# The second MLP matrix converted later, with a two-step threshold, wider loads of the mixed rows and one more buffer in two rings

## The chip, the cores and the metric

One core of a Trainium2 chip runs one program, start to end. The metric is the device time of one execution in microseconds (us), the median over the runs shown. The engines are named as the profile names them: PE (TensorE, with PEld for its weight loads), DVE (VectorE), ACT (ScalarE), POOL (GpSimd) and SP (SyncE), whose queue issues nearly every DMA of this program.

## The reference

The input `x` has 8 sequences of 3136 positions and 256 channels. Two layers are computed in float32:

```python
X = np.fft.rfft(x, axis=1)
Yr = Xr @ w_r - Xi @ w_i + b_r;  Yi = Xr @ w_i + Xi @ w_r + b_i
Y* = sign(Y*) * max(|Y*| - 0.01, 0)            # soft threshold
y  = np.fft.irfft(Yr + 1j * Yi, n=3136, axis=1)

mixed = real(fft(fft(y, axis=1), axis=2));  u = y + mixed
un = (u - mean(u)) / sqrt(var(u) + 1e-6)
out = u + max(un @ w_ch1, 0) @ w_ch2           # 256 -> 1024 -> 256
```

The MLP matrices `w_ch1` and `w_ch2` reach the program as raw 8-byte words and are turned on the chip into pairs of float32 values, a high and a low part.

## The kernel before

**Work and stages.** All heavy products are matrix multiplies on PE. Float32 accuracy comes from splitting an operand into a high part (type fp32r) and a low part (the remainder) and adding three products, `mm3` (L154 to L157). Eight sequences `b` go through three stages. Stage 1 (`p1`, L371) does the first half of a Fourier transform over positions (49 x 64 positions) and stores it to DRAM (`ad`). Stage 2 works in four quarters `q` of 8 frequencies each: `p2_f2` (L438) finishes the transform and makes the tiles Xh, Xl (and sums Xsh, Xsl), `p2_w` (L510) multiplies by the complex weights, adds the bias and applies the soft threshold into `Y`, `p2_mix` (L553) does the transform over channels and stores `mq` to DRAM as `md`, `p2_yt` and `p2_g2` (L648, L686) begin the inverse transform and store `bev` to DRAM as `bd`. Stage 3 takes groups of 3 or 4 position tiles: `p3_norm` (L718) loads `bf` from `bd` and `mt` from `md`, ends the inverse transform in PSUM (`g_g`), adds `mt` into `ut` and computes mean and variance; `p3_tr` transposes `ut` into `uth`, `utl`; `p3_mlp1` and `p3_mlp2` are the MLP (`h`, then `o`), and the result leaves from `ut`.

**Order.** Each stage of each sequence is a Python generator that yields a due time in units of T; a heap calls the one that is due next, and a scheduler that simulates the engines then fixes the order of every engine's instructions. At run time each engine follows its own fixed order and waits for semaphores. Stage 1 of the first sequence fills the time 0 to 1 T, stage 2 of the first sequence begins at 1 T, that of the second at 1.77 T (START1), stage 3 of sequence 0 at about 2 T. From there on the stages of neighbouring sequences overlap.

**The conversion.** `weights()` (L845) has eight pieces: four of `w1` (due from 1.14 T, L127) and four of `w2` (due from 1.56 T, step 0.05 T, L128). A piece loads 512 KB of raw words (L858) and runs `split_double` (L170): one ACT instruction (L179), six on DVE (L180, L182, L184, L185, L188, L190), a copy on ACT (L194) and two subtractions or additions on POOL (L196, L197). Its scratch tiles use the rings `mt` and `ut`. The raw words of `w2` lie in the tiles Xh and Xl (one buffer each), which hold the spectra of even quarters at other times. Behind the four pieces of `w1`, `center()` (L262) takes the mean out of it.

**The threshold.** `p2_w` adds bias and the product `ks` to the product in PSUM with one DVE instruction that writes `y1` (L544), clips `y1` to [-0.01, 0.01] into `m` (L546, DVE), and subtracts (L547: on DVE for the first sequence and where `o` is 0, else on POOL). PSUM has 8 banks: 4 for the tag `g` (every product outside the MLP), 2 for `h`, 2 for `o`.

**Loads of the mixed rows.** `p3_norm` loads `mt` for each pair of tiles: per source one DMA for the rows in rising order (L750) and one for each tile of the falling rows (L752), into a ring of 2 buffers.

Of the kernel before, what the change touches and what calls it, by code (L numbers as in the profile page):

```python
# [133 lines left out]
def spectral_block(ctx: ExitStack, tc: tile.TileContext, x, w_ri, b_ri, w1, w2,  # L134
# [78 lines left out]
    def load_consts():  # L213
# [504 lines left out]
    def p3_norm(b):  # L718
# [7 lines left out]
        def load_bf(m, n):  # L726
# [5 lines left out]
            return bf  # L732
        nxt = None
        for gi, (g0, z) in enumerate(groups[b % 2]):
            t0, T3 = clock3(b, g0)
            for i, n in parts_of[z]:
# [10 lines left out]
                mt = sb.tile([128, 2, D], F32, tag="mt", bufs=2, name="mt")  # L747
                for r, (bb, n2) in enumerate(sources(m)):
                    mpn, mmn = (d[0:NH].rearrange("(a n2) d -> a n2 d", n2=N2) for d in m_dram[bb])
                    nc.sync.dma_start(out=mt[32 * r:32 * r + 32, :n], in_=mpn[:, n2:n2 + n, :])  # L750
                    for j in range(n):
                        nc.sync.dma_start(out=mt[64 + 32 * r:96 + 32 * r, j], in_=mmn[:, 48 - n2 - j, :])  # L752
                if b and gi == i == 0:
                    yield t0 + T3 * (NRM + TURN)
# [8 lines left out]
                va.tensor_add(ut[:, :n], g[:, :w].rearrange("p (n d) -> p n d", d=D), mt[:, :n])  # L763
# [163 lines left out]
```

## Time and profile before

| what | value |
|---|---|
| median of the runs shown | 1908.15 us (three runs: 1908.15, 7055.32, 1907.27) |
| the profiled execution's own time | 1905.15 us |
| its span, first to last instruction | 1903.4 us |
| PE busy | 1838.9 us (97%) |
| DVE, ACT, POOL busy | 1255.0, 847.7, 706.1 us (66%, 45%, 37%) |
| mean granted TensorE clock | 0.983 |

The page cuts the span into 40 slices of 47.6 us. In the first four, PE is busy 5, 7, 7 and 6 tenths and the granted clock stands at 7, 9, 9 and 6 tenths; from the fifth slice on both are 9 tenths or more. A line with "[3.22 <-POOL ...]" says how long the engine sat idle before that instruction and what ended the wait. Matmuls are pipelined, and their busy times overlap.

### The profile page before, as it was taken

What the parts mean: (1) busy time and instruction counts of PE and PEld (TensorE: products, weight loads), DVE (VectorE), ACT (ScalarE), POOL (GpSimd) and SP (SyncE); (2) the same over time, 40 slices, a digit from 0 to 9 for tenths busy, and PEclk for the clock granted to TensorE, in tenths of its full rate; (3) what the DMA queues carried; (4) which work ended last, traced back from release to release, by engine and by line L of the source; (5) the groups of instructions that cost most, each with busy time, mean ns of one, the idle gap of its engine ahead of it and who ended that gap; (6) DMA issues with size and microseconds to landing.
All of it is one profiled execution on the core that took longest, in us unless ns stands there. A gap on an engine that the chain in (4) does not pass through costs nothing.

```text
span 1903.4 us, 34682 instructions
## 1 busy us (share of the span) xinstructions
PE 1838.9 (97%) x12123; PEld 1690.0 (89%) x12123; DVE 1255.0 (66%) x2726; ACT 847.7 (45%) x1892; POOL 706.1 (37%) x1093
## 2 busy tenths in 40 slices
PE   5776999999999999999999999999999999999999
PEld 4665999999999999989999999998999999998998
DVE  2885877767666766767766766766766776665443
ACT  2554545444544444444444544444454443443322
POOL 0565544343434334344323544324443332323110
PEclk7996999999999999999999999999999999999999
DMA  7775643354433545245443543435434342224110
GB/s 205 213 207 164 162 136 116 103 162 135 124 115 109 151 120 149 83 121 145 121 143 94 160 134 107 127 92 158 140 99 114 100 116 83 73 77 117 58 38 26
DMA packets 163716, 233.03 MB, mean 122 GB/s; under 512 B 27662, under 2 KB 107606, under 8 KB 163542
## 3 DMA queue, kind: packets, MB, share of 16 engines
q1 hardware_dynamic: 163542, 230.82, 42.8%
q8 instruction: 96, 1.57, 0.3%
q14 instruction: 78, 0.64, 0.1%
HBM read 127.95 MB, written 102.76 MB: 121 GB/s over the span
## 4 chain that ended last, share of the span: by engine, by line
PE 84%; DMA 5%; DVE 5%; SPq 2%; ACT 1%; issue 1%; POOL 1%; DVEq 0%; ACTq 0%; POOLq 0%
PE o L156 9%; PE o L155 9%; PE h L155 9%; PE o L157 9%; PE h L157 9%; PE h L156 9%; PE g_f L478 5%; PE g_w L155 3%; PE g_w L157 3%; PE g_w L156 3%; PE g_g L155 2%; PE g_yt L673 2%; PE g_g L156 2%; PE g_g L157 2%; PE g_ut L797 2%; PE g_mix L604 1%
## 5 line engine op out<-in xcount | busy, mean ns | idle before, releaser
L819 DVE SCALAR_TENSOR_TENSOR hl<-h,hh 128x512 fp32r<-128x512 f32 (+1 forms) x416 | 273.1, 657 | 335.9 <-ACT hh L818 334.2
L818 ACT ACTIVATE hh<-h 128x512 fp32r<-128x512 f32 (+1 forms) x416 | 238.5, 573 | 465.0 <-PE h L157 430.3
L156 PE MATMUL o<-w2h,hl 128*128 128x256 f32 x1568 | 427.7, 283 | 4.7 <-DVE hl L819 4.4
L157 PE MATMUL o<-w2h,hh 128*128 128x256 f32 x1568 | 421.6, 279 | 0.0
L155 PE MATMUL o<-w2l,hh 128*128 128x256 f32 x1568 | 391.2, 284 | 0.6 <-ACT hh L818 0.6
L155 PE MATMUL h<-utl,w1h 128*128 128x512 f32 (+1 forms) x832 | 324.4, 390 | 0.0
L157 PE MATMUL h<-uth,w1h 128*128 128x512 f32 (+1 forms) x832 | 317.7, 382 | 0.0
L156 PE MATMUL h<-uth,w1l 128*128 128x512 f32 (+1 forms) x832 | 317.4, 381 | 0.0
L156 PEld LDWEIGHTS o<-w2h,hl 128*128 128x128 f32 x1568 | 295.4, 188 | 11.2 <-DVE hl L819 6.1
L157 PEld LDWEIGHTS o<-w2h,hh 128*128 128x128 f32 x1568 | 295.2, 188 | 3.6
L155 PEld LDWEIGHTS o<-w2l,hh 128*128 128x128 f32 x1568 | 282.6, 189 | 12.8 <-ACT hh L818 0.8
L152 POOL TENSOR_TENSOR bl<-bf,bh 128x512 fp32r<-128x512 f32 x104 | 129.1, 1241 | 289.9 <-ACT bh L757 286.4
L152 POOL TENSOR_TENSOR xl<-xf,xh 128x512 fp32r<-128x512 f32 (+1 forms) x75 | 99.7, 1329 | 210.5 <-ACT xh L405 198.2
L157 PEld LDWEIGHTS h<-uth,w1h 128*128 128x128 f32 x832 | 156.3, 188 | 23.9
L155 PEld LDWEIGHTS h<-utl,w1h 128*128 128x128 f32 x832 | 156.6, 188 | 14.2
L156 PEld LDWEIGHTS h<-uth,w1l 128*128 128x128 f32 x832 | 156.7, 188 | 14.0
L478 PEld LDWEIGHTS g_f<-tff,af 98*128 98x128 f32 x1024 | 144.5, 197 | 19.8 <-issue 11.9
L478 PE MATMUL g_f<-tff,af 98*128 98x100 f32 x1024 | 151.0, 276 | 9.7 <-DMA tff<-c_tf 9.3
L152 POOL TENSOR_TENSOR Xl<-xx,Xh 128x400 fp32r<-128x400 f32 (+1 forms) x96 | 101.9, 1063 | 92.0 <-ACT Xh L492 42.2
L152 POOL TENSOR_TENSOR Xsl<-xs,Xsh 128x200 fp32r<-128x200 f32 x120 | 76.1, 635 | 103.4 <-ACT Xsh L492 90.8
L763 DVE TENSOR_TENSOR ut<-g_g,mt 128x512 f32<-128x512 f32 x104 | 68.3, 657 | 69.1 <-PE g_g L157 40.9
L772 POOL TENSOR_SCALAR vv<-ag 128x2 f32<-128x2 f32 x104 | 27.2, 261 | 205.4 <-DVE ag L769 182.7
(162 smaller groups left out, 3788.2 us busy)
## 6 DMA issues: line engine op xcount, KB each, us to landing
bd<-bev SPq DMA_DIRECT2D x128, 196.0 KB
bf<-bd SPq DMA_DIRECT2D x184, 128.0 KB
out_dram<-ut SPq DMA_DIRECT2D x92, 256.0 KB
af<-ad SPq DMA_DIRECT2D x60, 392.0 KB
xf<-in_x SPq DMA_DIRECT2D x176, 128.0 KB
ad<-ev SPq DMA_DIRECT2D x176, 128.0 KB
md<-mq SPq DMA_DIRECT2D x112, 192.0 KB
mt<-md SPq DMA_DIRECT2D x416, 32.0 KB
```

The source lines that it names most:

```text
L152: gp.tensor_sub(out_, full, hi.bitcast(F32))
L155: te.matmul(o, lh, rl, start=start, stop=False)
L156: te.matmul(o, ll, rh, start=False, stop=False)
L157: return te.matmul(o, lh, rh, start=False, stop=stop)
L478: f2_mm[b, q, ui] = te.matmul(o, afs[s][:, ui * D + k * 128:ui * D + k * 128 + 128], tfs[s][:, ui].rearrange("p (c j) -> p c j", c=2), sta ...
L604: te.matmul(o, eh[:, e, ui], cs, start=e == 0, stop=False)
L673: te.transpose(gt[:100, (v * 2 + o) * 128:(v * 2 + o + 1) * 128], y[:, o, place].rearrange("p c j -> p (c j)"), ident)
L763: va.tensor_add(ut[:, :n], g[:, :w].rearrange("p (n d) -> p n d", d=D), mt[:, :n])
L772: gp.tensor_scalar(vv[:, :n], ag[:, :n, 1:2], 1.0, EPS, op0=ALU.mult, op1=ALU.add)
L797: te.transpose(gv[:, k, j * 128:(j + 1) * 128], ut[:, j, k * 128:(k + 1) * 128], ident)
L818: sc.activation(hh[:, :w], h[:, :w], AF.Relu)
L819: va.scalar_tensor_tensor(hl[:, :w], h[:, :w], 0.0, hh[:, :w].bitcast(F32), op0=ALU.max, op1=ALU.subtract)
```

## The change

- The soft threshold becomes two DVE instructions and one on ACT. L545 (numbers of the changed file) adds bias and `ks` and writes the sum back into the same PSUM tile; ACT makes r = max(sum - 0.01, 0) from PSUM (L549); DVE takes min(sum + 0.01, r) into `Y` (L550). POOL has no part in it any more. `y1` and `m` are gone.
- `mt` is loaded once for a group of up to 4 tiles (`load_mt`) into one buffer, a quarter of a group's time ahead of its use, and the falling rows of a group in one DMA with a negative step; the first group is loaded in two cuts.
- The ring `ut` has 7 buffers in place of 6, `bev` 3 in place of 2.
- The pieces of `w2` are due from 1.73 T in steps of 0.07 T. Their raw words lie in `uth` and `utl`, two buffers each, so that all four fit at a time; those tiles hold the spectra of quarters 1 and 3 of the first sequence before, and the transposed `ut` of stage 3 after. The scratch tile of a conversion is in the ring `hh`.

```diff
-W2_AT, W2_STEP = 1.56, 0.05
+W2_AT, W2_STEP = 1.73, 0.07
...
-    UTB = 6
+    UTB = 7
...
-        tf = tmp("mt", 2, F32)
+        tf = tmp("hh", 2, F32)
...
+    va.memset(lam_t, -LAM)
...
-                    y1 = sb.tile([128, 8, S], F32, tag="y1", bufs=2, name="y1")
-                    va.scalar_tensor_tensor(y1, gw, bias[:, c, o:o + 1], ks, op0=ALU.add, op1=ALU.add)
-                    m = sb.tile([128, 8, S], F32, tag="m", bufs=1, name="m")
-                    va.tensor_scalar(m, y1, -LAM, LAM, op0=ALU.max, op1=ALU.min)
-                    (va if b == 0 or o == 0 else gp).tensor_sub(y[:, o, :, c, :], y1, m)
+                    va.scalar_tensor_tensor(gw, gw, bias[:, c, o:o + 1], ks, op0=ALU.add, op1=ALU.add)
...
+                    r = sb.tile([128, 8, S], F32, tag="r", bufs=1, name="r")
+                    sc.activation(r, gw, AF.Relu, bias=lam_t)
+                    va.scalar_tensor_tensor(y[:, o, :, c, :], gw, LAM, r, op0=ALU.add, op1=ALU.min)
...
-                bev = sb.tile([98, 512], F32, tag="bev", bufs=2, name="bev")
+                bev = sb.tile([98, 512], F32, tag="bev", bufs=3, name="bev")
...
+        def load_mt(g0, z):
+            mt = sb.tile([128, 4, D], F32, tag="mt", bufs=1, name="mt")
+            cut = 2 if g0 == 0 else z - 1 if g0 + z == NM else z
+            for i, n in ((0, cut), (cut, z - cut))[:1 + (cut < z)]:
+                for r, (bb, n2) in enumerate(sources(g0 + i)):
+                    mpn, mmn = (d[0:NH].rearrange("(a n2) d -> a n2 d", n2=N2) for d in m_dram[bb])
+                    nc.sync.dma_start(out=mt[32 * r:32 * r + 32, i:i + n], in_=mpn[:, n2:n2 + n, :])
+                    nc.sync.dma_start(out=mt[64 + 32 * r:96 + 32 * r, i:i + n],
+                                      in_=mmn[:, 49 - n2 - n:49 - n2, :][:, ::-1])
+            return mt
...
+            if gi:
+                yield t0 + T3 * (NRM - 0.25)
+                mt = load_mt(g0, z)
...
-            tag, bufs = (("W2", "W3") if j < 4 else ("Xh", "Xl"))[j % 2], 1
+            tag, bufs = (("W2", "W3") if j < 4 else ("uth", "utl"))[j % 2], 1 + j // 4
...
-            if j + 1 < 4 or j >= 4 and j + 1 < 8:
+            if j + 1 < 4 or 4 < j < 7:
                 load(j + 1)
...
                 load(4)
+                load(5)
```

The scheduler moves many instructions. Three places matter here.

The DVE queue where the conversion of `w2` begins, in the kernel before; `cv_w_...` are its scratch tiles, `raw_w` its raw words, `y`, `m` and `Y` the threshold of quarter 3, and `mq` the channel mix of quarter 2:

```order
L271 TENSOR_TENSOR wc<-w1h,g_mean 128x512 x2
L184 TENSOR_SCALAR cv_w_ut<-raw_w_1169 128x512
L623 COPY mq<-mq 100x4x127
L544 SCALAR_TENSOR_TENSOR y_1210<-g_w,bias,ks 128x400
L180 TENSOR_SCALAR cv_w_mt<-cv_w_mt 128x512
L546 TENSOR_SCALAR m<-y_1210 128x400
L182 TENSOR_SCALAR cv_w_mt<-cv_w_mt 128x512
L409 COPY ev<-g_f_1241 128x512
L547 TENSOR_TENSOR Y<-y_1210,m 128x8x50
L185 TENSOR_TENSOR cv_w_ut<-cv_w_ut,cv_w_mt 128x512
```

And the same queue in the changed kernel, around the last threshold of quarter 3:

```order
L545 SCALAR_TENSOR_TENSOR g_w<-g_w,bias,ks 128x400
L550 SCALAR_TENSOR_TENSOR Y<-g_w,r 128x8x50
L617 TENSOR_TENSOR mq<-g_mix,mq 100x1
L620 TENSOR_TENSOR mq<-mq 100x4x64 x2
L585 SCALAR_TENSOR_TENSOR ef<-Y,mask 128x8x25 x2
L184 TENSOR_SCALAR cv_w_ut<-raw_w_1342 128x512
L180 TENSOR_SCALAR cv_w_hh<-cv_w_hh 128x512
L182 TENSOR_SCALAR cv_w_hh<-cv_w_hh 128x512
L185 TENSOR_TENSOR cv_w_ut<-cv_w_ut,cv_w_hh 128x512
L626 COPY mq<-mq 100x4x127
```

Before, all four pieces stand among the thresholds of quarter 3 and ahead of that quarter's `mq`; now no piece stands ahead of the last threshold, three stand ahead of quarter 3's `mq`, and the fourth behind it.

The SP queue where the raw words of `w2` are loaded, in the changed kernel; `af` is the input of the second sequence's stage 2, `bd` the store of the first sequence's inverse transform:

```order
L288 DMA xf<-in_x 64x512 x3
L460 DMA af<-ad_107 98x1024
L709 DMA bd_109<-bev 98x512
L288 DMA raw_w_1342<-in_w 128x2x512
L288 DMA raw_w_1344<-in_w 128x2x512
L288 DMA tif<-c_ti 100x392
L460 DMA af<-ad_107 98x1024
L709 DMA bd_109<-bev 98x512
L288 DMA raw_w_1521<-in_w 128x2x512
L288 DMA raw_w_1579<-in_w 128x2x512
```

The four loads stand close together, and the first can only issue once quarter 3's products have read `uth`; before, two stand behind quarter 2's products and the others each wait for a piece that is done.

The DVE queue at the first normalisation of stage 3, in the changed kernel; `ut` is the sum of the inverse transform and `mt`, `st` and `ag` its statistics, and `raw_w_1579` the fourth piece of `w2`:

```order
L545 SCALAR_TENSOR_TENSOR g_w<-g_w,bias,ks 128x400 x2
L550 SCALAR_TENSOR_TENSOR Y<-g_w,r 128x8x50
L776 TENSOR_TENSOR ut<-g_g_1662,mt 128x512
L776 TENSOR_TENSOR ut<-g_g_1690,mt 128x512
L184 TENSOR_SCALAR cv_w_ut<-raw_w_1579 128x512
L781 BN_STATS st<-ut 128x6
L550 SCALAR_TENSOR_TENSOR Y<-g_w,r 128x8x50
L781 BN_STATS st<-ut 128x6 x3
L185 TENSOR_TENSOR cv_w_ut<-cv_w_ut,cv_w_hh 128x512
```

Before, this stretch had the same work without any piece of the conversion in it.

## Rows read from the trace of the kernel before

**Rows 1.** Engines by stretch of the span: busy us (instructions), clock, DMA.
```profile
core 0: us, PE busy (x) PEld busy (x) DVE busy (x) ACT busy (x) POOL busy (x), PEclk, DMA share, GB/s
62.00:84.00 22.00, 17.17 (x95) 13.18 (x94) 22.00 (x41) 13.37 (x33) 13.77 (x15) 1.00 0.72 204
84.00:121.00 37.00, 35.04 (x197) 28.54 (x195) 27.01 (x57) 20.13 (x58) 21.04 (x25) 1.00 0.61 175
121.00:152.00 31.00, 19.56 (x90) 14.84 (x91) 30.66 (x49) 16.84 (x36) 20.21 (x13) 0.81 0.70 205
152.00:167.00 15.00, 11.40 (x59) 9.86 (x60) 7.96 (x16) 10.00 (x27) 10.02 (x9) 0.73 0.71 199
167.00:191.00 24.00, 16.32 (x56) 14.06 (x55) 9.99 (x24) 8.26 (x15) 10.77 (x20) 0.63 0.55 154
200.00:600.00 400.00, 400.00 (x2703) 371.50 (x2702) 284.26 (x621) 190.03 (x424) 163.45 (x247) 1.00 0.45 128
1100.00:1350.00 250.00, 249.00 (x1668) 229.81 (x1667) 172.54 (x373) 115.79 (x256) 100.40 (x147) 1.00 0.43 122
```

**Rows 2.** Waits of PE from 200 us on: us in total, times, longest.
```profile
PE o L156 <- DVE hl L819: 4.4, 4, 1.4
PE g_yt L673 <- DVE utl L149: 0.7, 1, 0.7
```

**Rows 3.** DVE groups in 50 to 134 us: busy us, mean ns of one, idle before.
```profile
L547 DVE TENSOR_TENSOR Y<-y,m 128x400 f32<-128x400 f32 x14 | 11.9, 853 | 0.2
L544 DVE SCALAR_TENSOR_TENSOR y<-g_w,bias,ks 128x400 f32<-128x400 f32 x13 | 8.2, 628 | 2.5 <-PE g_w L157 2.5
L546 DVE TENSOR_SCALAR m<-y 128x400 f32<-128x400 f32 x14 | 8.0, 573 | 0.2
```

**Rows 4.** DVE in order of time, 120 to 166 us: start, us.
```profile
120.78 0.43 DVE L184 TENSOR_SCALAR cv_w_ut<-raw_w 128x512 int32<-128x512 int32 x1 [3.50 <-DMA raw_w<-in_w]
...
122.33 0.36 DVE L546 TENSOR_SCALAR m<-y 128x400 f32<-128x400 f32 x1
...
127.82 1.43 DVE L546 TENSOR_SCALAR m<-y 128x400 f32<-128x400 f32 x1
...
165.47 1.21 DVE L623 COPY mq<-mq 100x508 f32<-100x508 f32 x1
```

**Rows 5.** POOL in order of time, at 127 us.
```profile
127.58 1.44 POOL L196 TENSOR_TENSOR cv_w_ut<-cv_w_ut,w2h 128x512 f32<-128x512 f32 x1
```

**Rows 6.** The conversion's tiles cv_w_ut, then cv_w_mt, in 121 to 152 us.
```profile
121.00:152.00 31.00, 12.47 (x16) 2.47 (x4) 10.10 (x7) 0.81 0.70 205
...
121.00:152.00 31.00, 8.17 (x12) 2.49 (x4) 0.81 0.70 205
```

**Rows 7.** Groups of the whole span by shape, on ACT and POOL.
```profile
L547 POOL TENSOR_TENSOR Y<-y,m 128x400 f32<-128x400 f32 x56 | 63.1, 1127 | 107.7 <-DVE m L546 105.7 <-DMA mt<-md 1.1
L535 ACT COPY ks<-g_w 128x400 f32<-128x400 f32 x64 | 31.5, 493 | 37.6 <-PE g_w L157 37.3
```

**Rows 8.** PE in order of time, 133 to 191 us.
```profile
133.16 0.34 PE L157 MATMUL g_w<-Xh,wdh 128*128 128x400 f32 x1
...
178.85 0.79 PE L155 MATMUL g_g<-bl,invh 128*128 128x512 f32 x1 [3.22 <-POOL Y L551]
...
185.15 1.11 PE L797 MATMUL g_ut<-ident,ut 128*128 128x128 f32 x4 [3.80 <-DVE ut L763]
...
191.03 0.39 PE L155 MATMUL h<-utl,w1h 128*128 128x512 f32 x1
```

**Rows 9.** SP's DMA issues in order of time, 114 to 175 us.
```profile
114.98 0.92 SPq L286 DMA_DIRECT2D raw_w<-in_w  x2
...
167.85 0.51 SPq L629 DMA_DIRECT2D md<-mq  x1
...
173.31 1.26 SPq L730 DMA_DIRECT2D bf<-bd  x2
```

**Rows 10.** DVE group of the sum from PSUM, in 600 to 1600 us.
```profile
L544 DVE SCALAR_TENSOR_TENSOR y<-g_w,bias,ks 128x400 f32<-128x400 f32 x69 | 43.3, 628 | 9.2 <-PE g_w L157 9.1
```

**Rows 11.** SP's waits over the span: us in total, times, longest.
```profile
SPq L750 <- DVE ut L763: 165.9, 53, 8.3
```

More of the change, by code (lines that the diff above doesn't have):

```diff
@@ L219, in load_consts @@
         behind("x", out=KF["wr"], in_=w_v[0])
-        wi = sb.tile([128, 2, D], F32, tag="mt", bufs=2, name="wi")
+        wi = sb.tile([128, 2, D], F32, tag="mt", bufs=1, name="wi")
         behind("x", out=wi, in_=w_v[1])
@@ L237, in load_consts @@
         sc.copy(cs[:, 0, 1, 0:1], t[:, 0, 128:129])
-        inv = sb.tile([128, 128], F32, tag="mt", bufs=2, name="inv_f")
+        inv = sb.tile([128, 128], F32, tag="mt", bufs=1, name="inv_f")
         nc.sync.dma_start(out=inv, in_=c_inv)
@@ L254, in spectral_block @@
         va.memset(t[:, :, 0:1], 0.0)
-    eps_t = cp.tile([128, 1], F32, name="eps_t")
+    two_t = cp.tile([128, 2], F32, name="two_t")
+    eps_t, lam_t = two_t[:, 0:1], two_t[:, 1:2]
     va.memset(eps_t, EPS)
+    va.memset(lam_t, -LAM)
     mlp_w = {}
@@ L542, in p2_w @@
                             done.add(("w", b))
-                    y1 = sb.tile([128, 8, S], F32, tag="y1", bufs=2, name="y1")
-                    va.scalar_tensor_tensor(y1, gw, bias[:, c, o:o + 1], ks, op0=ALU.add, op1=ALU.add)
-                    m = sb.tile([128, 8, S], F32, tag="m", bufs=1, name="m")
-                    va.tensor_scalar(m, y1, -LAM, LAM, op0=ALU.max, op1=ALU.min)
-                    (va if b == 0 or o == 0 else gp).tensor_sub(y[:, o, :, c, :], y1, m)
+                    va.scalar_tensor_tensor(gw, gw, bias[:, c, o:o + 1], ks, op0=ALU.add, op1=ALU.add)
+                    if b == q == o == c == 0:
+                        sb.tile([128, 32], F32, tag="gap", bufs=1, name="room")
+                    r = sb.tile([128, 8, S], F32, tag="r", bufs=1, name="r")
+                    sc.activation(r, gw, AF.Relu, bias=lam_t)
+                    va.scalar_tensor_tensor(y[:, o, :, c, :], gw, LAM, r, op0=ALU.add, op1=ALU.min)
             if q == 0:
@@ L746, in p3_norm @@
                 nxt = load_bf(*tiles[0]) if tiles else None
[L747 to L754, printed above, removed]
+                if gi == i == 0:
+                    mt = load_mt(g0, z)
+                    if b:
+                        yield t0 + T3 * (NRM + TURN)
                 bh = sb.tile([128, 512], F32R, tag="bh", bufs=2, name="bh")
@@ L762, in p3_norm @@
                 ut = sb.tile([128, 2, D], F32, tag="ut", bufs=UTB, name="ut")
[L763 removed]
+                va.tensor_add(ut[:, :n], g[:, :w].rearrange("p (n d) -> p n d", d=D), mt[:, i:i + n])
                 st = sb.tile([128, 2, 6], F32, tag="st", bufs=2, name="st")
```

## Prediction

> **What bounds the kernel now.** I read the engines by stretch first [rows 1]. From 200 to 600 us PE is busy 400.00 of 400, from 1100 to 1350 it is 249.00 of 250, both at the full clock of 2.4 GHz. The waits of PE from 200 us on [rows 2] are a handful; the largest sum is 4.4 us. So from about 191 us, where the first MLP product `h` runs [rows 8], to the end PE is the bound. The change adds no matrix product and takes none away, so those 1712 us can hardly become shorter. What can move is the start.
>
> There the same table shows DVE. In 62 to 84 us it is busy 22.00 of 22 while PE is busy 17.17. In 121 to 152 us it is busy 30.66 of 31 while PE has 19.56, at a clock of 0.81. From 152 to 191 us nobody is full: PE 11.40 of 15 and 16.32 of 24, clock 0.73 and 0.63. That is a chain of waits: quarter 3's last product at 133.16 us [rows 8], its `mq` copied at 165.47 us [rows 4], the `md` stores issued from 167.85 us and the second `bf` pair at 173.31 us [rows 9], PE's wait of 3.22 us for POOL at 178.85 us (the low part of `bf`; the row names the memset right behind it) and of 3.80 us for `ut` at 185.15 us [rows 8], and `h` at 191.03 us. PE's work of 121 to 191 us, each busy time multiplied by its clock, is 19.56 x 0.81 + 11.40 x 0.73 + 16.32 x 0.63 = 34.4 us at full clock. 70 - 34.4 = 35.6 us is all that can be had there, 4.8 us in 62 to 84 us, and 2.0 us in 84 to 121 us, where PE is busy 35.04 of 37.
>
> **The change part by part.** The sum is made against the profiled execution, 1905.15 us; the median of the runs stands 3.0 us above it, and I forecast the median.
>
> *Conversion of `w2`.* Its DVE work in 121 to 152 us is 12.47 + 8.17 = 20.64 us for four pieces [rows 6], 5.2 us a piece and two thirds of what DVE does there. In the new order no piece stands ahead of quarter 3's last threshold, three still stand ahead of quarter 3's `mq`, the fourth behind it. The three only change places with the thresholds; since DVE has no gap in the stretch, just the fourth leaves the path to `mq`: -5.2 us, with 0 as the other end (if PE, ACT or a transfer sets that end as soon as DVE gives way) and -12 us if the thresholds' earlier end also pulls forward what hangs on them.
>
> *The raw words.* Before, the first piece waits 3.50 us for them with DVE idle [rows 4], issued at 114.98 us and used at 120.78 us, 5.8 us later [rows 9, 4]. That idle time goes. Now their load issues behind quarter 3's last product. DVE has about 3.3 us of its own until it reaches the first piece (a sum, ACT's step, a minimum, two `mq` steps and two `ef`, by the durations below and some 0.75 us each for the pairs), so about 5.8 - 3.3 = 2.5 us of new idle time is late next. Behind that waiting instruction stand the copies that free the `g_mix` tiles, and PE's mix waits for them. Net -1.0 us; the ends are -3.5 (the loads land in time) and +2.5 us (the old wait was hidden).
>
> *The threshold.* Before: a sum of 628 ns, a clip of 573 and a subtraction of 853 [rows 3]. The last two come to 1.43 us. The new minimum reads one PSUM tile and one SBUF tile as the sum does, so I give it 0.63 us; it is not in this trace, and its bounds are the 628 ns of the sum and the 853 ns of the subtraction. ACT's step has the shape of the `ks` copy, 493 ns [rows 7]. In the new order sum and minimum often stand next to each other, so DVE idles up to 0.49 us in between. A product thus saves 1.43 - 0.63 = 0.80 us at best and 0.31 at worst; I take the middle, 0.55. Four products lie in 62 to 84 us and four in 121 to 152 us, where DVE is the bound: 8 x 0.55 = -4.4 us, ends -6.4 and 0 (the worst case with a minimum as long as the subtraction leaves 0.09 each).
>
> Why the old pair was long is seen in two rows: the same clip took 0.36 us at 122.33 us and 1.43 us at 127.82 us [rows 4], the latter while POOL ran a subtraction from 127.58 us for 1.44 us [rows 5]. The Trainium skill, SBUF — State Buffer, section "Who interferes with whom", says that a DVE instruction with two SBUF inputs, or in its two-port mode, can be blocked for the whole of a GpSimd instruction, and one with at most one SBUF input outside that mode is not. By that rule the minimum never stretches and its 0.63 us stands; were it to stretch as the subtraction did, the eight products would give back 8 x 0.22 = 1.8 us. The rows agree with the rule here. The skill's VectorE: DVE Perf Modes, section on the TRN2 errata, speaks against the gain: its cost of an instruction is 58 cycles from SBUF but 120 from PSUM, so without a GpSimd instruction beside them clip and subtraction are an estimated 0.27 + 0.48 us and the minimum 0.54, a gain of only 0.2 us, which ACT's step would eat; by it this term would be about 0.
>
> *A PSUM bank held longer.* It was free 0.63 us after the product; now after 0.63 + 0.49 + 0.63 = 1.75 us. In the first sequence, where PE has nothing but `g` tiles, some of the 16 products will stall PE: +1.5 us, ends 0 (no stall) and +6 (a third of 16 x 1.12).
>
> Later there is room. DVE runs 69 sums in 600 to 1600 us [rows 10], 16 to a sequence, so a sequence takes 232 us; it allocates about 125 `g` tiles (the loops of the three stages), one in 1.85 us, and with four banks one comes round after 7.4 us. 1.1 us more for 16 of 125 tiles should not be seen. There DVE saves little, POOL loses 63.1 us of subtractions [rows 7], ACT gains 112 x 0.49 = 55 us, and none of them is the bound. 0, ends -3 and +3 us.
>
> *The fourth piece in the first normalisation.* 5.2 us of DVE among the statistics of the first two tiles. DVE is busy 9.99 of 24 us there [rows 1], so most of it fits into waits: +1.0 us, ends 0 and +5.2.
>
> *Loads of `mt`, rings.* SP waits 165.9 us in total to reload `mt` [rows 11], off PE's path. Fewer DMAs and one more buffer for `ut` and `bev` shorten waits that other work covers; if that cover went, the 3.80 us before `ut` [rows 8] would show it. 0, ends -1 and +2.
>
> *The clock.* PE's instructions of 121 to 191 us lose 47.28 - 34.4 = 12.9 us to the lower clock, and the clock was lowest where PE waited most. Shorter waits should give back some: -1.5 us, ends 0 and -6.
>
> Sum: -5.2 - 1.0 - 4.4 + 1.5 + 0 + 1.0 + 0 - 1.5 = -9.6 us. 1905.15 - 9.6 = 1895.55, and with the 3.0 us to the median 1898.5 us.
>
> **The rivals.**
>
> *Nothing is gained.* The conversion stays ahead of quarter 3's `mq` with three of its four pieces, and between 152 and 191 us no engine is full, so transfers and SP's queue may set the end; the DMA engines are 0.71 busy at 152 to 167 us [rows 1], and the raw words of all four pieces now load behind 133 us. Against it speaks the DVE stretch without a gap. Price: the two DVE terms (9.6 us) go and the rest stays: 1908 us.
>
> *More is gained.* The thresholds of quarter 3 end without any conversion between them, and PE's transposes and the inverse transform follow at once, while DVE converts in what are now PE's stretches. From the last product to `mq` it took 165.47 - 133.16 = 32.3 us, some 10 us of it thresholds, pieces and stretched copies that would be gone. The -12 end of the first term with the -6 of the clock: -9.6 - 6.8 - 4.5 = -21 us, 1887 us.
>
> *Slower: the raw words come too late.* One mechanism at one place: SP issues in order and stops at the first raw load until quarter 3's last product; behind it stand the input of the second sequence's stage 2 and the stores of the inverse transform, and on DVE everything behind the first piece. For it speaks the position of the loads; against it that loads stood in SP's queue before as well. If the raw words cost their 5.8 us in full, the fourth piece its 5.2 us, the banks 1.5 us, and only the threshold's 4.4 us are gained, that is +8.1 us: 1916 us. It decides from a DVE wait above 5 us at the first piece.
>
> *Slower throughout.* If each of the 112 later products held PE for 0.4 us, 45 us: 1953 us. It needs tiles held longer than the 7.4 us above.
>
> **How the numbers follow.** Forecast 0.50 (1893 to 1904 us), nothing gained 0.20, more gained 0.13, raw words late 0.13, slower throughout 0.04. The range of 1884 to 1914 us takes in the first two, most of the third and the near half of the fourth, a good 0.85. A measurement of this kernel can tell about 2%, 38 us, from no change. Faster by that would take all that the start holds: 0.02. Slower by that is the last rival and a little: 0.05. Within: 0.93.
>
> **What would show it.** Right: `h` begins 8 to 12 us earlier; DVE in the stretch before quarter 3's last product no longer full; the minimum at about 0.63 us whether POOL works or not; a DVE wait of 2 to 3 us for raw words; PE from there on as full as before. Wrong: `h` at 191 us or later, PE waiting for the minimum in the later sequences, or a DVE wait for raw words above 5 us.

## The result and the profile after

| | before | after |
|---|---|---|
| median of the runs | 1907.71 us | 1891.78 us |
| profiled execution, its span | 1905.15, 1903.4 us | 1891.03, 1889.2 us |
| first `h` | 191.03 us | 183.99 us |
| from the first `h` to the end of the span | 1712.4 us | 1705.2 us |
| DVE, ACT, POOL busy | 1255.0, 847.7, 706.1 us | 1207.6, 918.2, 628.3 us |

The ratio of the two is 0.9914, with a 95% interval of 0.9898 to 0.9930: 16 us less, where 9.6 us less were forecast. It lies within the range and within 2%. The median before takes in one run of 7055.32 us; without it, it is 1907.27 us. Half of the 14.2 us that the span lost lies ahead of the first `h`, and half behind it, where I had put nothing.

The engines by stretch in the changed kernel (columns as in [rows 1]):

```profile
84.00:121.00 37.00, 36.01 (x209) 30.25 (x208) 23.43 (x51) 25.92 (x70) 18.62 (x24) 1.00 0.61 174
121.00:152.00 31.00, 23.90 (x137) 19.53 (x137) 20.96 (x41) 21.07 (x47) 16.95 (x13) 0.94 0.82 244
152.00:167.00 15.00, 5.00 (x19) 3.67 (x18) 11.16 (x17) 7.26 (x18) 12.98 (x12) 0.65 0.78 223
167.00:191.00 24.00, 20.79 (x99) 17.70 (x98) 16.24 (x37) 12.96 (x26) 13.27 (x21) 0.86 0.67 185
...
1100.00:1350.00 250.00, 250.00 (x1682) 230.50 (x1681) 158.80 (x356) 128.49 (x276) 89.11 (x139) 1.00 0.45 127
```

Against [rows 1], PE gained in 121 to 152 us (23.90 for 19.56, clock 0.94 for 0.81) and in 167 to 191 us (20.79 for 16.32, clock 0.86 for 0.63), and lost in 152 to 167 us, where it is busy 5.00 of 15 and POOL 12.98. At full clock the three stretches hold 23.90 x 0.94 + 5.00 x 0.65 + 20.79 x 0.86 = 43.6 us of PE's work against 34.4. DVE is full in none of them.

Of PE's waits from 200 us on, the one that led [rows 2]:

```profile
PE o L156 <- DVE hl L832: 0.4, 1, 0.4
```

The 4.4 us of [rows 2] for `hl` are 0.4. PE in order of time, as in [rows 8]:

```profile
130.16 0.34 PE L157 MATMUL g_w<-Xh,wdh 128*128 128x400 f32 x1
...
162.66 0.80 PE L155 MATMUL g_f<-xl,fwdh 128*128 128x512 f32 x1 [4.41 <-POOL xl L152]
...
174.38 0.66 PE L810 MATMUL g_ut<-ident,ut 128*128 128x128 f32 x4 [1.25 <-DVE ut L776]
176.25 0.66 PE L810 MATMUL g_ut<-ident,ut 128*128 128x128 f32 x4 [1.22 <-DVE ut L776]
...
183.99 0.48 PE L155 MATMUL h<-utl,w1h 128*128 128x512 f32 x1
```

The last product of quarter 3 comes 3.0 us earlier than in [rows 8]. The 3.80 us that PE waited there for the second `ut` are 1.22, with 1.25 for the first. New is 4.41 us of waiting for POOL at 162.66 us. DVE in order of time, as in [rows 4]:

```profile
137.81 0.43 DVE L184 TENSOR_SCALAR cv_w_ut<-raw_w 128x512 int32<-128x512 int32 x1 [3.32 <-DMA raw_w<-in_w]
...
160.77 0.71 DVE L626 COPY mq<-mq 100x508 f32<-100x508 f32 x1
...
173.63 0.69 DVE L776 TENSOR_TENSOR ut<-g_g,mt 128x512 f32<-128x512 f32 x1 [0.73 <-DMA mt<-md]
175.51 0.69 DVE L776 TENSOR_TENSOR ut<-g_g,mt 128x512 f32<-128x512 f32 x1 [1.19 <-DMA mt<-md]
...
178.57 0.57 DVE L550 SCALAR_TENSOR_TENSOR Y<-g_w,r 128x400 f32<-128x400 f32 x1 [1.70 <-ACT r L549]
...
180.73 1.25 DVE L149 TENSOR_TENSOR utl<-g_ut,uth 128x512 fp32r<-128x512 f32 x2
```

The wait for raw words is there, 3.32 us. The last `mq` copy comes at 160.77 us against 165.47 [rows 4]. The two `ut` stand 1.9 us apart. Then 5 us pass until `utl` is made, in which DVE waits 1.70 us for ACT's r. ACT makes r and `uth`, which `utl` needs:

```profile
177.43 0.62 ACT L770 CAST bh<-bf 128x512 fp32r<-128x512 f32 x1 [5.40 <-DMA bf<-bd]
...
178.44 1.06 ACT L812 CAST uth<-g_ut 128x512 fp32r<-128x512 f32 x2
```

In ACT's fixed order both `uth` stand, with r, behind a cast that waits 5.40 us for a later pair of `bf`, although PE transposes the second `ut` from 176.25 us on. PE has other work meanwhile: its longest wait between that and `h` is 0.46 us.

The minimum's DVE group in 50 to 131 us, as the group in [rows 3], and then ACT's part of the threshold over the span:

```profile
L550 DVE SCALAR_TENSOR_TENSOR Y<-g_w,r 128x400 f32<-128x400 f32 x15 | 8.5, 567 | 6.4 <-ACT r L549 6.4
```

```profile
L549 ACT ACTIVATE r<-g_w,two_t 128x400 f32<-128x400 f32 x128 | 76.2, 595 | 76.0 <-DVE g_w L545 70.8 <-DVE Y L550 2.5 <-DVE rs L786 2.0
```

The minimum takes 0.57 us, where clip and subtraction took 0.57 + 0.85 in [rows 3]. ACT's step takes 595 ns; I had taken the 493 ns of the `ks` copy [rows 7]. DVE waits for it as I supposed: 6.4 us over 15 minima, 0.43 each.

### The profile page after: what moved, and what is told of

It reads as the page before. It is cut to its first block, busy times and chain, and to the rows that moved or that the text cites. A ratio compares the mean times of both kernels' runs of the same rounds, so it can differ in the third digit from the quotient of the medians.

```text
span 1889.2 us, 34230 instructions
## 1 busy us (share of the span) xinstructions
PE 1832.5 (97%) x12123; PEld 1685.9 (89%) x12123; DVE 1207.6 (64%) x2655; ACT 918.2 (49%) x2020; POOL 628.3 (33%) x1037
## 4 chain that ended last, share of the span: by engine, by line
PE 89%; DMA 4%; DVE 2%; SPq 2%; issue 1%; ACT 1%; POOL 1%; DVEq 0%; ACTq 0%; POOLq 0%
PE o L155 9%; PE o L156 9%; PE h L155 9%; PE h L157 9%; PE h L156 9%; PE o L157 9%; PE g_f L480 5%; PE g_w L155 3%; PE g_w L157 3%; PE g_w L156 3%; PE g_yt L676 3%; PE g_g L155 3%; PE g_g L156 3%; PE g_g L157 3%; PE g_ut L810 2%; PE g_mix L607 1%
## 5 line engine op out<-in xcount | busy, mean ns | idle before, releaser
L152 POOL TENSOR_TENSOR bl<-bf,bh 128x512 fp32r<-128x512 f32 x104 | 128.6, 1237 | 309.1 <-ACT bh L770 305.1
L152 POOL TENSOR_TENSOR xl<-xf,xh 128x512 fp32r<-128x512 f32 (+1 forms) x75 | 96.8, 1291 | 228.7 <-ACT xh L407 226.5
L152 POOL TENSOR_TENSOR Xl<-xx,Xh 128x400 fp32r<-128x400 f32 (+1 forms) x96 | 99.7, 1042 | 93.9 <-ACT Xh L494 80.7
L152 POOL TENSOR_TENSOR Xsl<-xs,Xsh 128x200 fp32r<-128x200 f32 x120 | 77.3, 645 | 110.7 <-ACT Xsh L494 100.0
L549 ACT ACTIVATE r<-g_w,two_t 128x400 f32<-128x400 f32 x128 | 76.2, 595 | 76.0 <-DVE g_w L545 70.8
```

The lines of the kernel that those rows point to most:

```text
L152: gp.tensor_sub(out_, full, hi.bitcast(F32))
L549: sc.activation(r, gw, AF.Relu, bias=lam_t)
```

## Experiments

First the change was taken apart. Theory A: two sources, the conversion's move at the start and the rest behind it. B: the move alone. C: the rest alone. Medians of the kernel before were 1907.1, 1906.4 and 1906.9 us in the three series that follow.

**Late conversion alone.**

```diff
-W2_AT, W2_STEP = 1.56, 0.05
+W2_AT, W2_STEP = 1.73, 0.07
...
-        tf = tmp("mt", 2, F32)
+        tf = tmp("hh", 2, F32)
...
-            tag, bufs = (("W2", "W3") if j < 4 else ("Xh", "Xl"))[j % 2], 1
+            tag, bufs = (("W2", "W3") if j < 4 else ("uth", "utl"))[j % 2], 1 + j // 4
...
```

> The kernel before with the later conversion of w2 alone (due times 1.73 T and 0.07 T, raw words in uth and utl, scratch tile in hh); old threshold, old mt loads, old rings. Theory A (two sources): the start gives about 7 us through the conversion, the other 7 us come after 200 us from the rest; here 1900 us, first h at 184 to 187 us, PE idle after 200 us as in the kernel before (about 11 us). Theory B (all of it from the conversion's move): 1892 us and the later idle time gone too. Theory C (all of it from the combination; the move only shifts PE's idle time from 121-152 us to 152-167 us): 1906 to 1909 us, first h at 190 us or later.

Measured: 1903.17 us, ratio 0.9984 (0.9975 to 0.9992), 3 us less. First `h` at 187.47 us, then 1711.8 us to the end, as before. Its stretches of 121 to 167 us:

```profile
121.00:152.00 31.00, 22.00 (x119) 17.85 (x118) 24.51 (x42) 17.52 (x39) 14.89 (x11) 0.93 0.81 246
152.00:167.00 15.00, 10.64 (x38) 8.46 (x37) 12.42 (x20) 8.30 (x21) 12.11 (x12) 0.50 0.63 193
```

DVE is no longer full in 121 to 152 us, but PE's clock is 0.50 in the next stretch, where DVE and POOL now convert. The move does something, and only ahead of `h`; B falls, and the time lies between those of A and C.

**Threshold alone**, in the kernel before.

```diff
...
-                    va.scalar_tensor_tensor(y1, gw, bias[:, c, o:o + 1], ks, op0=ALU.add, op1=ALU.add)
-                    m = sb.tile([128, 8, S], F32, tag="m", bufs=1, name="m")
-                    va.tensor_scalar(m, y1, -LAM, LAM, op0=ALU.max, op1=ALU.min)
-                    (va if b == 0 or o == 0 else gp).tensor_sub(y[:, o, :, c, :], y1, m)
+                    va.scalar_tensor_tensor(gw, gw, bias[:, c, o:o + 1], ks, op0=ALU.add, op1=ALU.add)
...
+                    r = sb.tile([128, 8, S], F32, tag="r", bufs=1, name="r")
+                    sc.activation(r, gw, AF.Relu, bias=lam_t)
+                    va.scalar_tensor_tensor(y[:, o, :, c, :], gw, LAM, r, op0=ALU.add, op1=ALU.min)
```

> The kernel before with the two-step threshold alone. My prediction's term for it at the start was -4.4 us with +1.5 us for the banks, and nothing later: about 1904 us, first h 3 us earlier. Theory A: 1901 to 1904 us, where some of the later idle time goes as well. Theory B: 1907 us. Theory C: 1896 to 1900 us, the threshold being the largest part of the combination.

Measured: 1898.64 us, ratio 0.9965 (0.9952 to 0.9977), 6.7 us less, near C. But `h` begins at 191.22 us, no earlier than in the kernel before, and from there it takes 1897.5 - 191.22 = 1706.3 us, 6.1 us less. So the threshold gains nothing where I forecast its gain, and 6 us where I forecast none. In 62 to 84 us DVE does get room (busy 19.60 us of 22, for 22.00), but PE does no more there (16.36 us for 17.17): a full DVE was not what held PE in that stretch. The other four products lie before 152 us; here are the engines of that stretch, then the conversion's tiles `cv_w_ut` and `cv_w_mt` in it (columns DVE, ACT, POOL for the first, DVE, ACT for the second):

```profile
121.00:152.00 31.00, 21.78 (x86) 16.23 (x85) 30.28 (x44) 17.79 (x39) 18.64 (x15) 0.72 0.63 186
```

```profile
121.00:152.00 31.00, 14.18 (x15) 2.50 (x4) 9.55 (x8) 0.72 0.63 186
...
121.00:152.00 31.00, 10.98 (x12) 2.03 (x4) 0.72 0.63 186
```

DVE is as full as before. The conversion takes 14.18 + 10.98 = 25.2 us of it, against 20.6 in [rows 6]: 4.5 us more for the same pieces, and four products had 3.2 us to give. (From 110 to 160 us, the conversion takes 24 to 26 us in each of the six kernels with the new threshold and the conversion of `w2` in its old place, and 20.9 in the kernel before.) In DVE's order of time, and POOL's beside it:

```profile
122.17 0.41 DVE L180 TENSOR_SCALAR cv_w_mt<-cv_w_mt 128x512 f32<-128x512 f32 x1
...
125.59 1.48 DVE L180 TENSOR_SCALAR cv_w_mt<-cv_w_mt 128x512 f32<-128x512 f32 x1
127.00 1.50 DVE L188 TENSOR_SCALAR cv_w_ut<-cv_w_ut 128x512 int32<-128x512 int32 x1
...
130.43 0.56 DVE L550 SCALAR_TENSOR_TENSOR Y<-g_w,r 128x400 f32<-128x400 f32 x1
```

```profile
125.52 1.27 POOL L152 TENSOR_TENSOR xl<-xf,xh 128x512 fp32r<-128x512 f32 x1 [0.40 <-ACT xh L407]
126.75 1.46 POOL L152 TENSOR_TENSOR w1l<-wc,w1h 128x512 fp32r<-128x512 f32 x1
...
130.65 1.27 POOL L197 TENSOR_TENSOR w2l<-cv_w_ut 128x512 fp32r<-128x512 f32 x1 [1.03 <-DVE cv_w_ut L190]
```

The same L180 takes 0.41 us at 122.17 and 1.48 us at 125.59, beside POOL's 1.27 and 1.46 us; the minimum at 130.43, with POOL busy from 130.65, stays at 0.56, and none of the kernel's 128 minima took more than 0.58. The instructions that the threshold freed from lying beside POOL made room for the conversion's, which then lay beside it: so I read the trace, and no run tests it. The Trainium skill, SBUF — State Buffer, section "Who interferes with whom", says that instructions with one SBUF input outside the two-port mode are spared and copies and tensor-scalar instructions in that mode are not; these rows agree.

The bank that is held longer is a second candidate. PE, one row:

```profile
131.04 2.03 PE L703 MATMUL g_g<-yf,tif 100*98 100x256 f32 x4 [2.18 <-DVE Y L550]
```

The minimum at 130.43 us, for which PE waits here, stands behind five instructions of the conversion, 6.35 us in all, that DVE runs after the sum; before, the sum alone freed the bank. Quarter 3's last product runs at 137.91 us, 4.8 us later than in [rows 8]. No run tells the two apart.

**All but the late conversion**, against the changed kernel.

```diff
-W2_AT, W2_STEP = 1.73, 0.07
+W2_AT, W2_STEP = 1.56, 0.05
...
-            tag, bufs = (("W2", "W3") if j < 4 else ("uth", "utl"))[j % 2], 1 + j // 4
+            tag, bufs = (("W2", "W3") if j < 4 else ("Xh", "Xl"))[j % 2], 1
...
```

> The changed kernel with the conversion of w2 put back (due from 1.56 T in steps of 0.05 T, raw words in Xh and Xl), so threshold, mt loads and rings alone. Theory A: 1898 to 1901 us, first h at 188 to 191 us, PE idle after 200 us only about 6 us. Theory B: 1907 us. Theory C: 1892 us.

Measured: 1892.01 us, ratio 0.9931 (0.9919 to 0.9943); `h` at 185.88 us. That is C's number: without the later conversion the kernel is as fast as the changed one.

**Late conversion and threshold, without mt loads and rings:** the two diffs above, the first and the second, in the kernel before.

> The kernel before with the later conversion and the two-step threshold; old mt loads, ut ring of 6, bev ring of 2. Theory A: 1892 to 1896 us if the threshold removes the later idle time, 1898 to 1900 us if the mt loads and rings do. Theory B: 1892 us. Theory C: 1896 to 1900 us. First h at 184 us in A and B.

Measured: 1894.19 us, ratio 0.9938 (0.9926 to 0.9950), `h` at 186.06 us. On the threshold alone the late conversion is worth 5 us, on threshold, mt loads and rings nothing that shows. The time is the one that A gave for a threshold that removes the later idle time; no theory holds whole. Two edits reach for the same 5 us at the start. Which of mt loads and rings is the other?

**Threshold and mt loads, early conversion, old rings**, against the kernel with all but the late conversion.

```diff
-    UTB = 7
+    UTB = 6
...
-                bev = sb.tile([98, 512], F32, tag="bev", bufs=3, name="bev")
+                bev = sb.tile([98, 512], F32, tag="bev", bufs=2, name="bev")
```

> The changed kernel with the conversion of w2 put back and with the rings put back (ut 6, bev 2): two-step threshold and one load of mt for a group, scratch tile in hh. With rings of 7 and 3 it took 1892 us and h began at 185.9 us; the threshold alone took 1898.6 us and h began at 191.2 us. If the mt loads give those 5 us at the start (fewer DMA issues ahead of the second bf pair on SP): h at 186 us and 1892 to 1894 us. If the rings give them (the bd stores of bev are no longer held up): h at 190 to 191 us and 1897 to 1899 us.

Measured: 1892.91 us, ratio 0.9923 (0.9909 to 0.9937), `h` at 187.91 us.

**Threshold and rings, early conversion, old mt loads**, against the same kernel.

```diff
-            mt = sb.tile([128, 4, D], F32, tag="mt", bufs=1, name="mt")
+                mt = sb.tile([128, 2, D], F32, tag="mt", bufs=2, name="mt")
...
```

> The changed kernel with the conversion of w2 put back and with the old loads of mt: two-step threshold and rings of 7 and 3, scratch tile in hh. If the rings give the 5 us at the start: h at 186 us and 1892 to 1894 us. If the mt loads give them: h at 190 to 191 us and 1897 to 1899 us. If both this kernel and the one without rings have h at 186 us, it is the scratch tile in hh, which all of them share, or an order that any small shift brings about.

Measured: 1898.78 us, ratio 0.9959 (0.9945 to 0.9974), `h` at 191.24 us: the threshold alone over again. The rings give nothing; the mt loads do. What they do is seen on DVE at the first normalisation, first in the kernel before, then in the kernel with threshold and mt loads:

```profile
179.12 0.69 DVE L763 TENSOR_TENSOR ut<-g_g,mt 128x512 f32<-128x512 f32 x1 [2.00 <-DMA mt<-md]
...
182.01 0.69 DVE L149 TENSOR_TENSOR utl<-g_ut,uth 128x512 fp32r<-128x512 f32 x1 [1.19 <-ACT uth L799]
184.13 0.17 DVE L773 RECIPROCAL rs<-rs 128x2 f32<-128x2 f32 x1 [1.43 <-ACT rs L771]
184.41 0.69 DVE L763 TENSOR_TENSOR ut<-g_g,mt 128x512 f32<-128x512 f32 x1
```

```profile
179.27 0.68 DVE L776 TENSOR_TENSOR ut<-g_g,mt 128x512 f32<-128x512 f32 x1
...
181.25 0.66 DVE L776 TENSOR_TENSOR ut<-g_g,mt 128x512 f32<-128x512 f32 x1
...
183.31 0.17 DVE L786 RECIPROCAL rs<-rs 128x2 f32<-128x2 f32 x1
```

Before, the second `ut` stands behind the first tile's `utl` and its reciprocal, which wait 1.19 and 1.43 us for ACT, and comes 5.3 us after the first. With the wide loads the scheduler puts it ahead of both, 2.0 us after the first. In the order of the two programs:

```
threshold alone:         ut  ...  RECIPROCAL rs  ut  ...  RECIPROCAL rs
threshold and mt loads:  ut  ...  ut  ...  RECIPROCAL rs  ...  RECIPROCAL rs
```

PE's wait of 3.80 us [rows 8] was for this second `ut`. The distance follows the loads in every profile: 4.4 to 5.3 us in the seven with the old ones, 1.5 to 2.1 us in the seven with the wide ones. But it is not all that sets `h`: with late conversion and threshold, `h` begins at 186.06 us although PE waits 4.53 us for the second `ut`.

**The issues moved**, in the kernel with the threshold alone. I first took that wait for one for `mt` itself.

```diff
+                two = b == gi == 0
+                for ii, nn in (parts_of[z] if two and i == 0 else [] if two else [(i, n)]):
...
+                    mts[ii] = mt
+                mt = mts[i]
```

> The kernel with the two-step threshold alone, old mt loads and old rings, in which only one thing is moved: the mt loads of the first group's second pair of tiles are issued with those of the first pair, ahead of the third bf pair on SP. Theory M (the 5 us that the wider mt loads give at the start are the wait of the second ut for its mt rows, which SP issues behind the third bf pair): second ut 2 us behind the first in place of 4.4 us, h at 187 to 189 us in place of 191.2 us, 1893.5 to 1896.5 us against 1898.6 us. Rival (the number of DMAs or their width counts, or one load for the whole group later on): h at 191 us, 1897 to 1900 us.

Measured: 1899.84 us, ratio 0.9967 (0.9954 to 0.9980), as the threshold alone. But the profiled run is the slowest of its seven, 1905.53 us, with `h` at 195.01 us: outside what theory M and the rival had put for it. SP does issue the loads ahead of the third `bf` pair (the last `mt`, then `bf`), and DVE's order is the old one:

```profile
182.71 0.88 SPq L757 DMA_DIRECT2D mt<-md  x2
183.69 1.23 SPq L733 DMA_DIRECT2D bf<-bd  x2
```

```profile
182.93 0.68 DVE L770 TENSOR_TENSOR ut<-g_g,mt 128x512 f32<-128x512 f32 x1
...
187.05 0.17 DVE L780 RECIPROCAL rs<-rs 128x2 f32<-128x2 f32 x1 [0.92 <-ACT rs L778]
187.32 0.69 DVE L770 TENSOR_TENSOR ut<-g_g,mt 128x512 f32<-128x512 f32 x1
```

The second `ut` starts 4.4 us after the first, right behind the reciprocal that waited 0.92 us. So my theory M falls: an earlier issue without the new place on DVE gained nothing here. That the place alone, with narrow loads, would gain the 5 us was not tried. In this profile the first `bf` load issues at 168.17 us against 164.05 with the threshold alone, and the first `ut` is 3.4 us late; it is read for the distance of the two `ut`. The edit also puts the third `bf` pair at 183.69 us, 6.2 us later than with the threshold alone, so it moves more than the `mt` issues.

**POOL's subtractions put back beside the new threshold.** Is the 6 us behind `h` DVE's own time, or POOL's?

```diff
+                    if b and o:
+                        yv = y[:, o, :, c, :]
+                        dm = sb.tile([128, 8, S], F32, tag="dm", bufs=1, name="dm")
+                        gp.tensor_sub(dm, yv, yv)
```

> The kernel with the two-step threshold alone, and in it the 56 subtractions that POOL ran before put back as idle work: POOL subtracts a piece of Y from itself into a tile that nothing reads, at the places where it ran the old subtraction. The threshold alone took 6 us out of the time after the first h, all of it there. Theory D (what went is DVE's own time: two instructions of 0.63 and 0.57 us in place of 0.63, 0.57 and 0.85 us, so hl stands behind less): 1897 to 1901 us, PE's wait for hl below 1 us in all. Theory P (what went is POOL's subtraction beside DVE, which held up DVE's instructions and with them hl): 1903 to 1907 us, PE's wait for hl back at 3 to 5 us.

Measured: 1909.35 us, ratio 1.0016 (1.0007 to 1.0026): the gain is gone and 3 us more, from the first `h` on 1716.2 us. DVE's L585 (here L589) makes the mix's operands from Y; the group with the threshold alone, then with POOL's work put back, in 200 to 1850 us:

```profile
L585 DVE SCALAR_TENSOR_TENSOR eo<-Y,mask 128x200 f32<-128x200 f32 x109 | 51.6, 508 | 0.5
```

```profile
L589 DVE SCALAR_TENSOR_TENSOR eo<-Y,mask 128x200 f32<-128x200 f32 x110 | 77.1, 733 | 0.4
```

PE's waits for `hh` and `hl` from 200 us on in this kernel:

```profile
PE o L155 <- ACT hh L825: 4.9, 3, 2.0
...
PE o L156 <- DVE hl L826: 0.3, 1, 0.3
```

The minimum keeps its 570 ns, L589 goes from 508 to 733. Neither theory holds: the time lies 2 us above P's range and 8 above D's, and PE waits 4.9 us for `hh` and 0.3 for `hl`, which was D's mark and not P's. At the two longest of these waits, 1.97 us at 839.19 and 1.82 us at 1291.87, `hh` stands on ACT behind copies of `eo` that wait for DVE:

```profile
833.31 4.94 DVE L589 SCALAR_TENSOR_TENSOR eo<-Y,mask 128x200 f32<-128x200 f32 x2
```

Elsewhere such a pair takes 0.75 us. POOL runs the mix's steps and low parts beside it (L626, L627, L152) and no idle subtraction. So the added work also acts through the order that the scheduler then chose. What the run shows is that 56 instructions of about 1 us on POOL, with that order, can cost PE 10 us behind `h`; it doesn't show that the old ones did it, nor by which wait.

For the kernel before, PE's four waits for `hl` can be read. DVE at two of them, in order of time:

```profile
831.56 2.35 DVE L149 TENSOR_TENSOR el<-eo,eh 128x400 fp32r<-128x400 f32 x1 [0.26 <-ACT eh L588]
...
834.43 1.90 DVE L623 COPY mq<-mq 100x508 f32<-100x508 f32 x1
...
1072.23 0.69 DVE L763 TENSOR_TENSOR ut<-g_g,mt 128x512 f32<-128x512 f32 x1 [4.42 <-DMA out_dram<-ut]
1072.84 0.55 DVE L819 SCALAR_TENSOR_TENSOR hl<-h,hh 128x384 fp32r<-128x384 f32 x1
```

At 1073.44 us, and in the same way at 620.49, `hl` stood behind a `ut` that waited 4.42 us (4.61) for its buffer to be stored: 2.5 of PE's 4.4 us. At 836.99 us, and in the same way at 1290.13, it stood behind an `el` of 2.35 us and an `mq` copy of 1.90, which take 0.56 and 0.42 elsewhere: 1.8 us. In the 6 us before each of the four, POOL runs none of the threshold's subtractions, so theory P is not what these rows show. The waits of `ut` for its store come to 10.2 us in 200 to 1850 us (5, the longest 4.6), and to 1.4 us (4, the longest 0.7) with the threshold alone, with the same ring of 6. They go with the threshold in all kernels: 9.2 to 13.0 us in the three profiles with the old one, 1.1 to 3.0 us in the eleven with the new one, and of these 1.1 us in the kernel with POOL's work put back. How the threshold shortens them, by POOL, by DVE's own time or by the order, stays open.

**The changed kernel with the old threshold** (and rings of 6 and 2, for its two tiles need the room).

```diff
...
-                    sc.activation(r, gw, AF.Relu, bias=lam_t)
-                    va.scalar_tensor_tensor(y[:, o, :, c, :], gw, LAM, r, op0=ALU.add, op1=ALU.min)
+                    va.tensor_scalar(m, y1, -LAM, LAM, op0=ALU.max, op1=ALU.min)
+                    (va if b == 0 or o == 0 else gp).tensor_sub(y[:, o, :, c, :], y1, m)
...
```

> The changed kernel with the old threshold (clip and subtraction, POOL's 56 among them), rings of 6 and 2; late conversion and wide mt loads stay. Theory P and M (two separate gains: POOL's subtraction gone is worth 6 us after the first h, the mt loads 5 us before it): h at 185 to 188 us, time after h again 1711 to 1713 us, PE's wait for hl 3 to 6 us, 1898 to 1902 us. If the threshold's gain depended on nothing but luck in the order: 1893 to 1896 us.

Measured: 1901.36 us, ratio 0.9964 (0.9950 to 0.9978), `h` at 188.44 us, 1714.1 us from there. PE's wait for `hl` from 200 us on:

```profile
PE o L156 <- DVE hl L829: 4.4, 4, 1.7
```

The 4.4 us for `hl` are back, and the time behind `h`; `h` and that time each lie up to 1.1 us beyond what was expected. So the threshold's gain stands beside the other edits too. The three kernels with the old threshold (before, late conversion alone, this one) took 1711.8 to 1714.1 us behind `h`, all those with the new one and no added POOL work 1705.2 to 1708.8 (each from one profile).

**The changed kernel once more**, with no edit.

> The changed kernel once more, beside the others, to place the later conversion's share on top of the rest: 1889 to 1892 us. If the later conversion is worth its 2 us in h (184.0 against 185.9 us), 1890 us, 2 us below the kernel without it; if it gives nothing on top, 1892 us.

Measured: 1893.45 us, ratio 0.9928 (0.9915 to 0.9941), `h` at 186.27 us. Against the kernel before, the kernels with the conversion put back stand at 0.9923 in this series and 0.9931 in the one ahead of it. The later conversion's share on top of the rest is nothing that can be told. The same kernel has `h` at 183.99 in one profile and at 186.27 us in the other, so a difference of 2 us in `h` between two kernels says nothing. PE's work in 121 to 191 us, 43.6 us in the first profile, is 41.2 in the second.

**Part of the conversion earlier instead.** In the changed kernel DVE has room in 84 to 121 us, where PE is full (36.01 of 37, DVE 23.43). The mt tile, now 4 KB wide and free until the first normalisation, can hold raw words there. The edit of the kernel with three pieces:

```diff
...
+            tag = ("W2", "W3", "W2", "W3", "mt", "mt", "mt", "Xl")[j]
...
+        load(4)
+        yield T * 1.39
+        piece(4)
+        load(5)
+        yield T * 1.45
+        piece(5)
+        load(6)
...
```

> The changed kernel with the conversion of w2 neither late nor where it was: two of its pieces are converted at 1.42 T and 1.56 T from raw words in the mt tile, which is free until the first normalisation, the other two at 1.61 T and 1.66 T from Xh and Xl; the tables' scratch inv moves to hl. Theory E (84 to 121 us is PE's stretch, where DVE is busy 22 of 37 us, and 121 to 152 us is DVE's with 30 of 31; a piece moved from the one to the other takes 5.2 us off the path to mq, and POOL is not loaded in 152 to 167 us as in the late version): DVE 25 to 27 of 31 us in 121-152, h at 180 to 184 us, 1886 to 1890 us. Rival (the second bf pair and the mt loads set h whatever DVE does): h at 185 to 187 us, 1891 to 1894 us.

> As the kernel with two pieces early, but three of them through the mt tile (from 1.39 T, 1.45 T and 1.56 T) and only the last from Xl. Theory E: as much again or 1 to 3 us better, 1884 to 1889 us, unless the pieces now delay PE in 84 to 121 us (PE below 34 of 37 there), which would give it back. Rival: 1891 to 1894 us.

Measured: with two pieces 1890.75 us, ratio 0.9917 (0.9904 to 0.9931), `h` at 184.25 us; with three 1888.05 us, ratio 0.9904 (0.9891 to 0.9918), `h` at 180.97 us. The second kernel's stretches:

```profile
84.00:121.00 37.00, 32.57 (x180) 26.60 (x179) 25.82 (x53) 24.36 (x64) 20.77 (x25) 0.95 0.61 174
121.00:152.00 31.00, 26.64 (x140) 20.73 (x138) 24.67 (x42) 20.27 (x48) 21.44 (x15) 0.94 0.74 213
152.00:167.00 15.00, 9.79 (x56) 8.96 (x55) 8.07 (x15) 8.49 (x22) 9.09 (x9) 0.77 0.71 206
167.00:191.00 24.00, 20.11 (x109) 17.34 (x107) 16.08 (x35) 11.96 (x23) 9.80 (x19) 0.93 0.71 191
```

With two pieces the time lies between the two theories' ranges, with three in that of theory E. PE gives up some of 84 to 121 us: 32.57 of 37 at a clock of 0.95, 30.9 us of work for 36.0, below the mark of 34 from which the gain was to be given back. It has 26.64 x 0.94 + 9.79 x 0.77 + 20.11 x 0.93 = 51.3 us of work done in the next three, against 43.6 in the changed kernel: 7.7 us more for 5.1 given up. There is no hole as deep as the 5.00 of 15, though PE still waits 5.21 us for POOL's `xl` there. This is the lowest median of the case: its median is 4 to 5 us below the changed kernel's two, and its interval ends below that kernel's second ratio, 0.9928, though not below its first, 0.9914.

## Why the prediction was right, and where it wasn't

The direction held, and the time lies in the range; the size was 16 us for 9.6 (13 us in the second series, with 1893.45 us), and the terms that made it were mostly not those that I had summed. That they came to a sum within the range is in good part luck: a term of -4.4 us gave nothing at the start, and one put at 0 gave 6. The first time falls between the forecast's own band (1893 to 1904 us) and the rival "more is gained" (1887 us), the second just into the band, and by neither's account: no kernel shows the thresholds' earlier end pulling the start forward by itself.

- **Conversion, -5.2 us.** The step itself came as put: the fourth piece left the path, and the last `mq` copy came 4.7 us earlier. What it is worth in time depends on what else is there: 3 us alone, 5 beside the threshold, nothing beside threshold and mt loads. I had named the fourth piece's cost in the normalisation (1.0 us) but not the hole in 152 to 167 us, where PE waited 4.41 us for POOL and was busy 5.00 of 15. That the pieces dug it isn't shown: they hold POOL for 3.14 us there, against 2.23 before, and the kernel with three pieces early waits 5.21 us at the same place.
- **Raw words, -1.0 us.** The wait was 3.32 us for the forecast 2.5, below the 5 us from which the rival would have decided. Not measured by itself.
- **Threshold at the start, -4.4 us.** The step that failed. Measured alone, `h` did not move (191.22 for 191.03). The minimum was shorter than I took it (0.57 for 0.63) and never stretched, as forecast. But I took a full DVE for the bound in both stretches: in 62 to 84 us DVE got room and PE made nothing of it, and in 121 to 152 us I counted the 3.2 us of four products as free, where the conversion's instructions, stretched beside POOL, took 4.5 us more. By the errata section of the Trainium skill's VectorE: DVE Perf Modes the term would be about 0, as it was, but not for the reason it gives: in 50 to 134 us clip and subtraction took 1.43 us and the minimum 0.57, so the products did give something up. From 200 us on, clip and subtraction on DVE took 0.36 + 0.57 us in the kernel before, 0.37 more than the minimum, where its cycle table makes it an estimated 0.2; the section itself says that its row from SBUF comes out too short.
- **Threshold later, 0 (-3 to +3).** The largest miss. It took 6.1 us out of the time behind `h`. I had read PE's 4.4 us of waiting for `hl` [rows 2] as a handful and "none of them is the bound" as the end of the matter; a queue in fixed order can still hold PE up, and did. These waits went from 4.4 to 0.2 us with the threshold alone; all of PE's waits from 192 us on went from 6.1 to 2.3, so some 2 of the 6 us are in no wait that I can name.
- **PSUM bank, +1.5 us.** PE shows one wait for the minimum ahead of a stage 1 product, 1.1 us, in 62 to 152 us, and none behind `h`. Of the right size, but not measured against the old waits: before, PE waited 2.9 us for sums ahead of two `g_g` products in 121 to 140 us.
- **mt loads and rings, 0 (-1 to +2).** Right for the rings. Beside the threshold the mt loads gave 4 to 8 us (spans 1893.9 for 1897.5, ratios 0.9923 for 0.9965; `h` 3.3 us earlier). I had named the very wait, "the 3.80 us before `ut`", and taken it for one that would lengthen; I hadn't asked in which place of DVE's order that `ut` stood.
- **Clock, -1.5 us.** It rose where PE waited less (0.81 to 0.94, 0.63 to 0.86) and fell where it waited more (0.73 to 0.65). Right in direction; not measured apart.

Of the marks set beforehand, `h` came 7.0 and, in the second series, 4.8 us earlier, not 8 to 12; the DVE stretch did open; the minimum was as forecast; PE behind `h` was not "as full as before" but took 7.2 and 4.6 us less.

## What to carry to other kernels

A stall of a few us of an engine that is 99% busy is not a handful when the whole gain is 16: follow each back to what stands ahead in the fixed order of the engine waited for. Two edits that open the same gap don't add; take each out of the finished kernel, too, before crediting it. Look for the stretch in which the crowded engine has room under a full one, and move work there rather than merely later: here that gave the lowest median, though its interval still meets the changed kernel's.

## What the runs showed of the hardware

A threshold that takes 56 subtractions of 1.1 us off POOL, which is busy 37%, and 44 us off DVE was worth 6 us of PE's time behind `h`; which of these did it, or the new order, stays open. Idle work of that kind put back on POOL cost 10 us there, in an order of its own. DVE's conversion instructions of 128x512 with one SBUF input took 0.41 us alone and up to 1.50 us beside POOL, while the minimum, from PSUM and SBUF, took 0.53 to 0.58 us in all 128 cases of the changed kernel. A relu of a PSUM tile, with its bias read from a tile, took ACT 595 ns where a plain copy of a PSUM tile of the same shape took 493.
